# Batch one loaded in runs of four tokens with its last 64 apart, w_out by converting transfers of GpSimd's queue, batch three's loads behind it

## The chip, the cores and the metric

The kernel runs on one core of a Trainium2 chip. The core has five engines with a queue of instructions each: TensorE (matrix products and transposes, into PSUM), VectorE, ScalarE, GpSimd and SyncE (SP, which here only starts DMA transfers). Sixteen DMA engines move data between HBM and SBUF, whichever queue a transfer was started from. The metric is the device time of one execution in microseconds (us); lower is better.

## What is computed

Eight batches of eight heads, 576 tokens of 64 values each, go through attention within a window of 32 tokens to either side; the result, as 4608 tokens of 512 values, goes through a layer with a squared ReLU.

```python
scores = scale * np.matmul(q, k.transpose(0, 1, 3, 2))
mask = np.abs(pos[:, None] - pos[None, :]) <= 32
attn = softmax(np.where(mask, scores, -1e9))
x = np.matmul(attn, v).transpose(0, 2, 1, 3).reshape(4608, 512)
h = np.maximum(x @ w_in, 0.0)          # w_in 512 x 2048
out = (s * (h * h) + b) @ w_out        # w_out 2048 x 512
```

All inputs and the output are float32; the products run in bf16.

## The kernel before

The program is a list of tasks. `add` notes for each its engine (or the DMA queue that it is started on), an estimated cost, what it reads and writes, a key and explicit waits. `_Graph.plan` then puts the tasks of all engines into one order: each time it takes the task that can start first by its own model of engines and DMA rings, the lower key where two can start together. `_Graph.emit` turns dependencies across engines into semaphore waits. Each engine executes its tasks strictly in the planned order, so a wait on one holds up all behind it. Transfers have their order on SP's queue from rising keys (`nxt()`).

**Batches.** The code counts batches from 0; "batch one" is `b == 0`. Batches one to three are worked on by TensorE transposes of q and k; later batches use DMA transposes and are not touched by the change.

**Batch one.** `load_pair` (605) brings q or k of two heads, 576 tokens, as 128 partitions of nine tokens in a row (2304 bytes, `ROWS = 9`). `turn_pair` (618 to 640) casts to bf16 (622 and 623), transposes in eighteen 64x64 pieces (631) into a bank of `W`, and copies out into `QT` (ScalarE, 636) and `KT` (VectorE, 637). `pair_scores` (918) then makes the scores of one pair: two products add a large negative number where the window is shut (925), sixteen products of 64 key tokens by 128 query tokens go on top, and two more make the ninth key tile, with its 64 tokens, into `AVN`. An exp (946) per pair follows, one more for the ninth tile of all pairs, with a mask (951) behind it. `stir` (614) puts products of ones between them, whose results are overwritten; `STIR` says how many at which place.

**Units.** A unit is 128 query tokens, shifted by 32. `av_part` (843) multiplies exps with V, `finish` divides (865, 867), transposes (874) and copies to `XT` (882). Batch one has five units; the banks that they use are listed in `av_banks`. Unit four's keys take in key tile eight, unit five's key tiles eight and nine.

**Loads of batch one and two.** `ORDER0` orders SP's transfers behind q and k: V 0, then w_in part 0, V 1 to 4, w_in part 1. (Numbers are V tiles, 8 and 9 are w_in's parts; each part is two loads of 512 KB, cast by GpSimd at 564.) V comes in rows of 256 bytes, 256 KB a tile, 128 KB for the last. `ORDER1` continues with batch two: `part` (660, 672) loads the last 64 tokens ("t") and q and k of four heads in runs of four tokens (1024 bytes a row), casts (650), transposes in 128x128 pieces (664, 677) and copies out (655, 656); w_in's parts 2 and 3 and V stand between.

**w_out.** Behind batch two's V, eight loads of 512 KB go from SP's queue into the staging ring `STG` (561), and GpSimd casts each into `WOUT_BF` (564). `constant` (1213) sums w_out's rows on TensorE as they arrive; `weight_sums` (1111) makes four differences of its quarters on VectorE, one of them in place; `second` (1139) is the second layer, fourteen products per 512 tokens with these quarters. Behind w_out on SP's queue come batch three's q and k (`FOURS`, 660 and 672) and V.

**The hidden layer.** `s1` (1082) multiplies `XT` with w_in, ScalarE applies the ReLU (1089) and VectorE squares (1095). The first 512 tokens are cut into 224, 128 and 160 (`SPLIT`); the 224 need units one and two, and the order over w_in's parts is `FIRST`. The staging ring is shared by all loads of q, k and weights, so a load waits until the cast of what stood there before is done.

Of the kernel before, what the change touches and what calls it, by code (L numbers as in the profile page):

```python
# [7 lines left out]
BF16 = mybir.dt.bfloat16  # L8
AF = mybir.ActivationFunctionType
ALU = mybir.AluOpType  # L10

S = 576
# [15 lines left out]
ORDER0 = (0, 8, 1, 2, 3, 4, 9)  # L28
# [7 lines left out]
ROWS = 9  # L36
# [18 lines left out]
STIR = {("turn", 0, "q"): 7, ("scores", 0): 2, ("turn", 1, "q"): 1, ("turn", 1, "k"): 1, ("turn", 2, "q"): 1, ("turn", 2, "k"): 1,  # L55
        ("turn", 3, "k"): 1, ("scores", 2): 1, ("scores", 3): 2, ("av", 0): 2, ("av", 1): 1, ("av", 2): 1}
# [21 lines left out]
class _Graph:  # L78
# [44 lines left out]
    def plan(self):  # L123
# [10 lines left out]
        rings, clock, room = {"sp": [], "act": []}, [0.0], {}  # L134
# [188 lines left out]
def bass_sliding_window_symmetric__then__act_starrelu_kernel(  # L323
# [23 lines left out]
    with ExitStack() as es:  # L347
# [15 lines left out]
        def ps(shape, nm, dt=F32):  # L363
# [14 lines left out]
              for t in QTS]  # L378
# [35 lines left out]
                  "t": [f"dmaT{i}" for i in range(8)]}  # L414
# [135 lines left out]
        def load_weights(which, i, x, key, eng):  # L550

            stg, stgr = stage(2 * DM)
# [65 lines left out]
        def turn_pair(b, name, pr, key, banks, eng, slack):  # L618

            slot, (stg, stgr), ni = b % 2, land["pair", b, name, pr], take("nat", NNAT)  # L620
            nat = NAT[ni][:, 0:576]
            add(eng, (lambda e: e.copy(nat, stg)) if eng == "act" else
                (lambda e: e.tensor_copy(nat, stg)),
                {"act": 670.0, "dve": 420.0, "pool": 700.0}[eng], reads=stgr, writes=[("NAT", ni)],
                key=key, slack=slack)
            res, tile = banks[take("bank", len(banks))]
            if b == 0:
                stir(("turn", pr, name), res, tile, key)
            view = tile.bitcast(BF16)[:, 0:S].rearrange("p (i s) -> p i s", i=ROWS)
            order = view.rearrange("p i s -> p s i")  # L630
            add("pe", [lambda e, i=i, p0=p0: e.transpose(
                view[p0:p0 + 64, i, :], nat[p0:p0 + 64, i * 64:i * 64 + 64], IDENT[p0:p0 + 64, p0:p0 + 64])
                for i in range(ROWS) for p0 in (0, 64)], 600.0 if b == 0 and pr == 0 else 420.0, reads=[("NAT", ni), "IDENT"], writes=[res], key=key)
            flat = QT[slot][:, pr, WIN:WIN + S] if name == "q" else KT[slot][:, pr, :]
            dst = flat.rearrange("p (s i) -> p s i", i=ROWS)
            add(*(("act", lambda e: e.copy(dst, order), 190 + 0.833 * S) if name == "q" else
                  ("dve", lambda e: e.tensor_copy(dst, order), 60 + 1.04 * S)), reads=[res],
                writes=[({"q": "QT", "k": "KT"}[name], slot, x, pr) for x in range(NTILE)], key=key)

        def part(b, which, load_key, key, banks, slack):  # L640
# [6 lines left out]
            eng, out_eng = FCAST[which] if b == 1 else "act", FOUT[which]  # L647
# [10 lines left out]
            if which == "t":  # L658
# [3 lines left out]
                    for src, p0 in ((q, 0), (k, 64))], 1000.0, writes=stgr, key=load_key, dma=("l", 64, 21.5))  # L662
# [12 lines left out]
                600.0, writes=stgr, key=load_key, dma=("l", 32, 60.0))  # L675
# [233 lines left out]
        def pair_scores(b, pr):  # L909
# [21 lines left out]
            if tail:  # L931
                g.tasks[-1].deps.update(g.readers.get(("AVN", 0), []) + g.readers.get(("AVN", 1), []))
                for i in (0, 1):
                    g.writer["AVN", i], g.readers["AVN", i] = g.tasks[-1], []
# [9 lines left out]
        def first_exp(dst, src, np_, sc, res, key, shut=False):  # L944
# [3 lines left out]
            if shut:  # L948
                return
# [542 lines left out]
```

## Time and profile before

| | us |
|---|---|
| median of 3 runs (311.11 to 311.7) | 311.52 |
| the profiled execution | 313.66 |
| its span, first to last instruction | 311.9 |
| TensorE busy in it | 296.0 |
| VectorE, ScalarE, GpSimd busy | 230.5, 156.0, 64.0 |
| mean granted clock of TensorE | 0.982 of full |

A line of the timeline has start, duration, engine, source line, operation, what it writes and reads, and in brackets how long the engine was idle before it and what ended that. A line of the groups has the number of instructions behind an x, then busy time and the mean of one. "Issue" is a pause that ends with no event that the profile shows. PEclk gives the granted TensorE clock in tenths; a digit 9 is 90% or more. Ends of matrix products are modelled, since they are pipelined.

### The profile page before, as it was taken

The numbers are of one execution on the slowest core, as the hardware profiler recorded it, in microseconds if no ns is written. First come the engines' busy times: TensorE is split into PE (matmuls) and PEld (weight loads), VectorE is DVE, ScalarE is ACT, GpSimd is POOL, SyncE is SP. The second block draws the span as 40 slices with busy tenths as digits, with TensorE's granted clock in tenths as the row PEclk, the third lists the DMA queues.
The fourth block names the chain that finished last, engine by engine and source line by source line (L and its number), as shares of the span: only waits on it lengthen the run. The fifth ranks groups of instructions, "written<-read, shape, count | busy, mean of one in ns | idle before, by whom it ended". The sixth has DMA issues, their size and how long they took to land.

```text
span 311.9 us, 8962 instructions
## 1 busy us (share of the span) xinstructions
PE 296.0 (95%) x3906; PEld 215.9 (69%) x3938; DVE 230.5 (74%) x400; ACT 156.0 (50%) x241; POOL 64.0 (21%) x78
## 2 busy tenths in 40 slices
PE   8799988999999998999999999998999999999994
PEld 3458766788878886666666666666666666666783
DVE  3455777899799587789978786976786785666673
ACT  3655865494887653655655344443444433333300
POOL 5343558200000044027014300370000000000000
PEclk9967999999999999999999999999999999999999
DMA  7999899999495799999899879999812110200223
GB/s 233 302 258 354 225 302 291 284 272 241 112 198 148 193 188 177 247 219 201 196 230 199 140 177 277 189 179 165 151 53 84 52 48 5 98 25 11 68 69 105
DMA packets 118073, 54.32 MB, mean 174 GB/s; under 512 B 93760, under 2 KB 112832, under 8 KB 118032
## 3 DMA queue, kind: packets, MB, share of 16 engines
q1 hardware_dynamic: 118032, 53.72, 73.2%
q8 instruction: 32, 0.52, 0.7%
q14 instruction: 9, 0.07, 0.1%
HBM read 36.70 MB, written 9.44 MB: 148 GB/s over the span
## 4 chain that ended last, share of the span: by engine, by line
PE 80%; DMA 5%; DVE 4%; SPq 3%; issue 3%; ACT 2%; POOL 1%; POOLq 0%; ACTq 0%
PE w L1082 35%; PE o L1139 29%; DMA stg<-in_k_dram 4%; PE avn L843 4%; SPq L718 2%; PE sc L1139 2%; PE sc L785 2%; DMA kt<-nat 2%; PE avn L874 1%; POOL nat L737 1%; PE sc L1213 1%; DVE gt L1095 1%; PE o L843 1%; DVE kt L656 1%; PE sc L843 1%
## 5 line engine op out<-in xcount | busy, mean ns | idle before, releaser
L1082 PE MATMUL w<-xt,win 128*128 128x512 bf16 (+4 forms) x805 | 140.0, 315 | 3.8 <-issue 1.7
L1089 ACT ACTIVATE r<-w 128x512 bf16<-128x512 f32 (+2 forms) x148 | 86.6, 586 | 103.1 <-PE w L1082 101.7
L1082 PEld LDWEIGHTS w<-xt,win 128*128 128x128 bf16 x832 | 75.6, 99 | 36.3 <-ACT r L1089 1.9
L1095 DVE TENSOR_TENSOR gt<-r 128x1024 bf16<-128x1024 bf16 (+3 forms) x100 | 60.8, 617 | 34.5 <-ACT r L1089 33.8
L1139 PE MATMUL o<-wout,gt 128*128 128x256 bf16 x528 | 66.5, 273 | 0.0
L1139 PEld LDWEIGHTS o<-wout,gt 128*128 128x128 bf16 x528 | 51.2, 98 | 14.0
L737 POOL CAST nat<-stg 128x1024 bf16<-128x1024 f32 (+2 forms) x28 | 32.7, 1167 | 77.8 <-DMA stg<-in_q_dram 62.7
L813 ACT ACTIVATE ex<-sc 128x1024 bf16<-128x1024 f32 (+1 forms) x29 | 29.7, 1023 | 14.3 <-PE avn L843 13.3
L1139 PE MATMUL o<-tw,gt 128*128 128x256 bf16 x272 | 34.8, 273 | 0.0
L1155 DVE SCALAR_TENSOR_TENSOR outs<-o,sb,cvec 128x512 f32<-128x512 f32 (+1 forms) x36 | 25.8, 716 | 9.2 <-PE o L1139 9.2
L1139 PEld LDWEIGHTS o<-tw,gt 128*128 128x128 bf16 x272 | 26.1, 98 | 7.4
L817 DVE TENSOR_TENSOR ex<-ex,mask 128x1024 bf16<-128x1024 bf16 (+1 forms) x29 | 22.5, 777 | 3.5 <-ACT ex L813 3.0
L1155 DVE SCALAR_TENSOR_TENSOR outs<-o,sb,outs 128x512 f32<-128x512 f32 (+1 forms) x27 | 19.3, 713 | 7.2 <-PE o L1139 7.1
L1131 DVE TENSOR_TENSOR gt<-gt 128x1024 bf16<-128x1024 bf16 (+1 forms) x26 | 23.3, 896 | 0.3
L843 PE MATMUL avn<-vb,ex 64*64 64x65 bf16 x952 | 20.2, 199 | 1.8 <-DMA kt<-nat 0.8
L867 DVE TENSOR_TENSOR xn<-avn,rec 128x512 bf16<-128x512 f32 (+1 forms) x31 | 21.3, 686 | 0.6
L843 PEld LDWEIGHTS avn<-vb,ex 64*64 64x64 bf16 x952 | 13.1, 108 | 11.3 <-issue 5.6
L598 DVE CAST vb<-vst 128x512 bf16<-128x512 f32 (+1 forms) x30 | 13.5, 458 | 5.8 <-DMA vst<-in_v_dram 5.8
L1139 PE MATMUL o<-tw,gsum 128*128 128x256 bf16 x136 | 17.5, 273 | 0.0
L1139 PEld LDWEIGHTS o<-tw,gsum 128*128 128x128 bf16 x136 | 12.9, 98 | 3.1
L882 ACT COPY xt<-avn 128x512 bf16<-128x512 bf16 (+2 forms) x19 | 10.1, 539 | 7.9 <-PE avn L874 7.7
L1131 DVE TENSOR_TENSOR gsum<-gt 128x1024 bf16<-128x1024 bf16 x18 | 13.2, 734 | 0.3
(116 smaller groups left out, 226.7 us busy)
## 6 DMA issues: line engine op xcount, KB each, us to landing
vst<-in_v_dram SPq DMA_DIRECT2D x32, 256.0 KB, 4.6
out_dram<-outs SPq DMA_DIRECT2D x32, 256.0 KB, 2.9
stg<-in_q_dram SPq DMA_DIRECT2D x5, 1024.0 KB, 6.1
stg<-in_k_dram SPq DMA_DIRECT2D x20, 256.0 KB, 6.5
stg<-in_moe_w_in_dram SPq DMA_DIRECT2D x8, 512.0 KB, 7.4
stg<-in_moe_w_out_dram SPq DMA_DIRECT2D x8, 512.0 KB, 7.9
stg<-in_q_dram SPq DMA_DIRECT2D x4, 512.0 KB, 7.7
stg<-in_k_dram SPq DMA_DIRECT2D x4, 512.0 KB, 8.4
```

The source lines that it names most:

```text
L598: (lambda e: e.tensor_copy(VB[0:n, vb, :, 0:D], VST[0:n, vs, :, :])),
L737: (lambda e, dst=dst, src=src: e.tensor_copy(dst, src)),
L813: add("act", lambda e, dst=flat_dst, src=flat_src: e.activation(dst, src, AF.Exp, bias=0.0, scale=0.125), 190 + 0.833 * 512 * len(hs), rea ...
L817: add("dve", lambda e, flat=flat, mask=mask: e.tensor_tensor(flat, flat, mask, ALU.mult), 130 + 0.53 * 512 * len(hs), reads=[("E", ei, hp, ...
L843: return [lambda e: e.matmul(av[64 * x:64 * x + 64, h, 0:D + 1], lhsT=buf[64 * g:64 * g + 64, h % 2, h // 2, c:c + 64], rhs=VB[64 * g:64 * ...
L867: add("dve", lambda e: e.tensor_tensor(XN[xi][0:p1, :].rearrange("p (a c) -> p a c", a=H), av[0:p1, :, 0:D], REC[ri][0:p1, :].rearrange("p ...
L1082: add("pe", [lambda e, g=g, kc=kc: e.matmul(wt[:, g, :], lhsT=WIN_BF[:, kc, (f0 + g) * 128:(f0 + g + 1) * 128], rhs=XT[:, kc, t0 % XR:t0 % ...
L1089: add("act", lambda e: e.activation(rt, wt, AF.Relu, bias=0.0, scale=1.0), 190 + 0.833 * ng * nt, reads=[("W", wb)], writes=[("R1", rb, ha ...
L1095: add("dve", lambda e: e.tensor_tensor(GT[gs][:, f1:f1 + nf, g0:g0 + nt], rr, rr, ALU.mult), 130 + 0.55 * nf * nt, reads=[("R1", rb, x) fo ...
L1131: add("dve", lambda e: e.tensor_tensor(dst, x, y, op), 1240.0 if half is None else 690.0, reads=reads, writes=writes, key=k)
L1139: add("pe", [lambda e, g=g, j=j, dst=dst: e.matmul(dst, lhsT=lhs[:, g, 128 * j:128 * j + 128], rhs=rhs[:, g, :], start=first and g == 0 an ...
L1155: add("dve", lambda e, src=src, dst=dst, other=other: e.scalar_tensor_tensor(dst, src, SB128[:, 0:1], other, ALU.mult, ALU.add), 200 + 1.0 ...
```

## The change

Batch one's q and k are loaded by pairs of heads in runs of four tokens, 512 tokens in all (256 KB a load), cast with a rearrangement, transposed in four 128x128 pieces and copied out. The last 64 tokens of q and k of all heads come with one "t" part (two transfers, 256 KB in rows of 256 bytes) behind V 2, cast by GpSimd. The pairs' scores leave out the ninth key tile and the last 32 query columns of the eighth; `late_scores` makes both for all pairs in sixteen products into `AVN`, followed by two exps and two masks. Unit three uses `SC` in place of `AVN`. w_in part 1 moves ahead of V 4. The filler products change from 21 to 20, with one in place of four behind the last pair's scores.

w_out goes straight into `WOUT_BF` by eight converting transfers (float32 to bf16) on GpSimd's queue. The first two wait until V 2 of batch two has landed, the other six for its V 4. There is no staging and no cast. Batch three's five loads wait until the fifth of these has landed.

```diff
-ORDER0 = (0, 8, 1, 2, 3, 4, 9)
+ORDER0 = (0, 8, 1, 2, "t", 3, 9, 4)
-STIR = {("turn", 0, "q"): 7, ("scores", 0): 2, ("turn", 1, "q"): 1, ("turn", 1, "k"): 1, ("turn", 2, "q"): 1, ("turn", 2, "k"): 1,
-        ("turn", 3, "k"): 1, ("scores", 2): 1, ("scores", 3): 2, ("av", 0): 2, ("av", 1): 1, ("av", 2): 1}
+STIR = {("turn", 0, "q"): 7, ("scores", 0): 3, ("turn", 1, "q"): 2, ("turn", 1, "k"): 1, ("turn", 2, "q"): 1, ("turn", 2, "k"): 1,
+        ("turn", 3, "q"): 1, ("turn", 3, "k"): 1, ("scores", 2): 1, ("scores", 3): 1, ("av", 0): 1}
-        rings, clock, room = {"sp": [], "act": []}, [0.0], {}
+        rings, clock, room = {"sp": [], "act": [], "pool": []}, [0.0], {}
...
         def load_weights(which, i, x, key, eng):
+            if which == "out":
+                f0 = 4 * i + 2 * x
+                src = moe_w_out.rearrange("(fc p) c -> p fc c", p=128)[:, f0:f0 + 2, :]
+                dst = WOUT_BF[:, f0:f0 + 2, :]
+                add("pool", lambda e: e.dma_start(dst, src), 800.0, writes=[("W" + which, i, x)],
+                    key=EARLY + (1.25 if i == 0 else 2.0) + 0.01 * (i + 0.5 * x), waits=[land["v", 1, 2 if i == 0 else 4]],
+                    dma=("g", 16, 87.0))
+                land[which, i, x] = g.tasks[-1]
+                return
...
-        def load_pair(b, name, pr, load_key):
-            stg, stgr = land["pair", b, name, pr] = stage(S)
+        def load_pair(name, pr, load_key):
+            stg, stgr = land["pair", name, pr] = stage(DM)
             add("sp", lambda e: e.dma_start(
-                stg,
-                src_of[name][b, 2 * pr:2 * pr + 2, :, :].rearrange("h (p i) d -> (h p) (i d)", i=ROWS)),
-                600.0, writes=stgr, key=load_key, dma=("l", 8, 112.0 if b == 0 else 98.0))
+                stg.rearrange("p (h c) -> p h c", h=2),
+                src_of[name][0, 2 * pr:2 * pr + 2, 0:512, :].rearrange("h (p i) d -> p h (i d)", i=4)),
+                600.0, writes=stgr, key=load_key, dma=("l", 16, 60.0))
...
+            nat = NAT[ni][:, 0:512]
+            dst, src = nat.rearrange("p (i h d) -> p h i d", i=4, h=2), stg.rearrange("p (h i d) -> p h i d", h=2, i=4)
+            tile = tile.bitcast(BF16)[:, 0:512]
+            add("pe", [lambda e, i=i: e.transpose(tile[:, 128 * i:128 * i + 128], nat[:, 128 * i:128 * i + 128], IDENT[:, :])
+                       for i in range(4)], 260.0, reads=[("NAT", ni), "IDENT"], writes=[res], key=key)
...
-            eng, out_eng = FCAST[which] if b == 1 else "act", FOUT[which]
+            eng, out_eng = FCAST[which] if b < 2 else "act", FOUT[which]
...
-            name = ("SC", "O", "AVN", "SC", "O")[u] if b == 0 else BANK1[u] if b == 1 else "AVN"
+            name = ("SC", "O", "SC", "O", "AVN")[u] if b == 0 else BANK1[u] if b == 1 else "AVN"
...
+        def late_scores():
+            x, c = NTILE - 1, 128 - WIN
+            fns = []
+            for pr in range(NPAIR):
+                for hp in (0, 1):
+                    p = slice(64 * hp, 64 * hp + 64)
+                    fns.append(lambda e, pr=pr, hp=hp, p=p: e.matmul(
+                        AVN[0:64, hp, pr * 128:pr * 128 + 128], lhsT=KT[0][p, pr, 64 * x:64 * x + 64],
+                        rhs=QT[0][p, pr, 64 * x:64 * x + 128], start=True, stop=True))
+                    fns.append(lambda e, pr=pr, hp=hp, p=p: e.matmul(
+                        AVN[64:128, hp, pr * 128 + c:pr * 128 + 128], lhsT=KT[0][p, pr, 64 * x - 64:64 * x],
+                        rhs=QT[0][p, pr, 64 * x - 64 + c:64 * x + 64], start=True, stop=True))
+            key = -24.0
...
+            for u, p0, c0 in ((x // 2, 0, 0), (x // 2 - 1, 64, c)):
...
+                add("act", lambda e, dst=dst, src=src: e.activation(dst, src, AF.Exp, bias=0.0, scale=0.125),
+                    190 + 0.833 * 8 * (128 - c0), reads=[("AVN", 0), ("AVN", 1)], writes=res, key=key)
...
             for t in ORDER0:
-                if t < 8:
+                if t == "t":
+                    part(0, "t", nxt(), -23.5, banks, 200.0)
+                    late_scores()
+                elif t < 8:
...
                     for which in FOURS:
-                        part(b, which, nxt(), due(b, 0) - 4.0 + 0.1 * FOURS.index(which), banks2, 2500.0)
+                        part(b, which, nxt(), due(b, 0) - 4.0 + 0.1 * FOURS.index(which), banks2, 1500.0,
+                             [land["out", 2, 0]])
```

`part` takes the list as waits of its loads. Two slacks of the planner fall from 2500 to 1500 with it (here and in `piece`), which shifts the planned order of what uses these loads.

More of the change, by code (lines that the diff above doesn't have):

```diff
@@ L616, in stir @@
                     n * (427.0 if spot == ("turn", 0, "q") else 240.0), reads=["ONESW"], writes=[res], key=key - 0.05)
[L618 to L625, printed above, removed]
-            res, tile = banks[take("bank", len(banks))]
[L627 to L638, printed above, removed]
@@ L643, in part @@
+        def part(b, which, load_key, key, banks, slack, waits=()):
             slot, ni = b % 2, take("nat", NNAT)
@@ L935, in pair_scores @@
             for u0, n in ((0, 4),) if pr < NPAIR - 1 else ((0, 1), (1, 3)):
                 src = bank[:, :, 128 * u0:128 * (u0 + n)].rearrange("p h (u c) -> p h u c", c=128)
-                first_exp(EXS[:, u0:u0 + n, :, pr, :], src, 128, [(name, 0), (name, 1)],
-                          [("E", u, hp, pr) for u in range(u0, u0 + n) for hp in (0, 1)], key, True)
-            if pr == NPAIR - 1 and tail:
-                first_exp(EXS[0:64, 4, :, :, :].rearrange("p (one h) a c -> p (one a) h c", one=1),
-                          AVN[0:64, :, :].rearrange("p h (a c) -> p h a c", c=128), 64, [("AVN", 0), ("AVN", 1)],
-                          [("E", 4, hp, x) for x in range(NPAIR) for hp in (0, 1)], -24.5)
@@ L945, in first_exp @@
+        def first_exp(dst, src, sc, res, key):
             n = dst.shape[1]
```

60 lines of the change are left out of this document (34 added, 26 removed).

## The prediction

> **What bounds the kernel now.** I read the page first (engine shares, the slices, the chain of waits), then stages of the first 130 us, then TensorE's instructions with what ended each pause.
>
> ```profile
> span 311.9 us, 8962 instructions
> PE   8799988999999998999999999998999999999994
> PEclk9967999999999999999999999999999999999999
> DMA  7999899999495799999899879999812110200223
> PE 80%; DMA 5%; DVE 4%; SPq 3%; issue 3%; ACT 2%; POOL 1%; POOLq 0%; ACTq 0%
> q8 instruction: 32, 0.52, 0.7%
> ```
>
> TensorE fills nearly every slice and carries 80% of the chain; DMA is close to full until about 220 us. So the end is the moment from which TensorE is never out of work, plus its work, plus its pauses. The one stretch that is plainly wasted is in slices three and four, where its clock drops:
>
> ```profile
> 14.20:15.50 1.30, 0.04 (x2) 0.03 (x2) 0.00 (x0) 0.13 (x1) 0.52 (x1) 1.00 0.82 166
> 15.50:17.40 1.90, 1.83 (x45) 0.92 (x45) 0.21 (x1) 1.40 (x3) 1.17 (x2) 0.97 0.82 186
> 17.40:20.80 3.40, 3.25 (x74) 1.98 (x73) 2.67 (x7) 1.58 (x3) 1.10 (x2) 0.50 0.97 260
> 20.80:24.10 3.30, 3.16 (x68) 2.28 (x67) 2.37 (x7) 1.17 (x2) 2.08 (x2) 0.50 1.15 301
> 24.10:27.50 3.40, 3.40 (x27) 3.02 (x25) 0.62 (x3) 1.71 (x4) 1.18 (x2) 0.50 1.07 349
> 46.00:50.00 4.00, 3.86 (x92) 3.23 (x90) 3.87 (x9) 1.65 (x4) 2.94 (x3) 1.00 1.05 394
> ```
>
> Columns are the stretch, its length, busy time of TensorE, weight loads, VectorE, ScalarE and GpSimd, the granted clock, the DMA share and GB/s. From 17.4 to 27.5 us the clock is half, while TensorE is busy 9.8 of 10.1 us: at full clock that work takes about 5 us less. The drop follows an empty 1.3 us and a stretch of 64-row products; the granted clock is at 9 and more again in the fifth slice, after 24.1 to 27.5, the first stretch of dense 128x128 products. From the eighth slice (55 us) on TensorE's digits are nines, so what is won ahead of it should reach the end.
>
> **The front: loads and turning.** Batch one's q and k come in eight loads of 256 KB for eight of 288 KB.
>
> ```profile
> 5.00:10.00 5.00, 4.96 (x116) 2.87 (x114) 2.24 (x5) 2.27 (x3) 1.73 (x4) 1.00 1.02 333
> 15.00:20.00 5.00, 4.28 (x101) 2.31 (x101) 2.37 (x6) 2.98 (x5) 2.16 (x3) 0.73 0.86 195
> 20.00:25.00 5.00, 4.86 (x92) 3.71 (x93) 2.99 (x9) 1.28 (x3) 2.80 (x4) 0.50 1.10 322
> 9.49 0.47 PE L631 MATMUL w<-ident,nat 64*64 64x64 bf16 x18
> 28.08 0.39 PE L664 MATMUL avn<-ident,nat 128*128 128x128 bf16 x4
> 13.03 0.76 DVE L637 COPY kt<-w 128x576 bf16<-128x576 bf16 x1 [0.84 <-PE w L631]
> 15.50 0.42 PE L918 MATMUL o<-qt,kt 64*64 64x128 bf16 x16 [1.26 <-issue]
> 51.80 0.22 PE L874 MATMUL o<-ident,xn 128*128 128x128 bf16 x1 [1.23 <-issue]
> ```
>
> 256 KB less ahead of V and w_in at 333 GB/s is 0.8 us. Rows shrink from 2304 to 1024 bytes; batch two already moves such rows (20 to 27.5 us, 301 to 349 GB/s), so I price that at nothing; at the 195 GB/s of the V stretch the 2 MB would come 3.4 us later, the upper bound. Four 128x128 transposes (0.39) replace eighteen of 64x64 (0.47), and a copy of 512 columns is 8/9 of 0.76: 0.2 us off the last pair's own chain. The 1.26 us pause before the last pair's scores is no wait for data (k was ready at 13.79). A second one stands inside a group of four transposes. The program's code arrives in 32 pieces (the instruction queue), and I take both for a late piece. There are 112 transposes fewer, so 224 instructions with their weight loads, and the pause must move; if it vanishes it is worth up to 1.26. But units two and three wait for V, which moves by 0.8 alone: I take **-0.8** for the front, bounds -2.3 (0.8 + 0.2 + 1.26) and +3.4 - 0.8 = +2.6.
>
> **The last 64 tokens.** Their load of 256 KB in 256-byte rows stands behind V 2, w_in's second part before V 4.
>
> ```profile
> 17.27 0.62 POOL L598 CAST vb<-vst 128x512 bf16<-128x512 f32 x1 [0.71 <-DMA vst<-in_v_dram]
> 17.48 1.02 ACT L946 ACTIVATE ex<-avn 64x1024 bf16<-64x1024 f32 x1
> 18.53 0.68 DVE L951 TENSOR_TENSOR ex<-ex,mask 64x1024 bf16<-64x1024 bf16 x1 [0.41 <-ACT ex L946]
> 19.50 0.61 POOL L598 CAST vb<-vst 64x512 bf16<-64x512 f32 x1 [1.61 <-DMA vst<-in_v_dram]
> 20.90 0.94 PE L843 MATMUL sc<-vb,ex 64*64 64x65 bf16 x32
> 22.31 0.93 PE L843 MATMUL o<-vb,ex 64*64 64x65 bf16 x24
> 21.00 0.59 ACT L882 COPY xt<-o 128x512 bf16<-128x512 bf16 x1 [1.36 <-PE o L874]
> 23.18 1.68 PE L1082 MATMUL w<-xt,win 128*128 128x224 bf16 x8
> 26.89 1.35 PE L1082 MATMUL w<-xt,win 128*128 128x128 bf16 x16
> 29.03 0.39 ACT L655 COPY kt<-avn 128x256 bf16<-128x256 bf16 x1
> ```
>
> V 2 lands at 17.2 now, so near 16.4; the tail 1.3 us later (256 KB at 195 GB/s), 17.7. Then, one after the other: GpSimd's cast 0.61, four transposes at half clock 0.6, ScalarE's two copies 0.8, sixteen products 0.6, two exps (1.02, and a quarter of the columns, about 0.4), two masks (0.68 and about 0.3): 5.0 us, so 22.7, and with hand-overs about 23. Both the fourth unit's key tile and the fifth's depend on it (20.90 and 22.31 now), and V 4 waits behind 1 MB of w_in (3.3 us at 322 GB/s): 19.5 - 0.8 + 1.3 + 3.3, cast at 23.3. These two units are about 2 us late. What covers it is the hidden layer's first products: they need units one and two (copied out by 21.6 now, 20.8 then) and w_in's first part, and take twice 1.68 and 1.35, 4.7 us at half clock. I cost it at nothing; without that cover 2 us.
>
> **The clock.** Those dense products move from 23.2 to about 20.5, ahead of the late units, so the 20.8 to 24.1 stretch is filled as 24.1 to 27.5 is now, and the clock should come back one such stretch earlier: 3.4 us at full instead of half, **-1.7**. Bounds: -3.4 (two) to +1.7 (one more, if they start late). [...]
>
> **Filler products.** Behind 15.5 us they fall from four to one.
>
> ```profile
> 15.90 0.61 PE L614 MATMUL sc<-onesw 128*128 128x512 bf16 x2
> 17.14 0.52 PE L614 MATMUL o<-onesw 128*128 128x512 bf16 x1
> 18.92 0.63 PE L614 MATMUL avn<-onesw 128*128 128x512 bf16 x1
> ```
>
> That is 0.3 + 0.52 + 0.63 = 1.45 less; the tail's transposes (0.6) and products (0.6 less the 0.25 that its eight small ones took within the pairs) give 0.95 back: **-0.5**, bounds -1.45 and 0, since the gaps left may only be waits for V.
>
> **w_out.** Eight loads from SP with a cast each on GpSimd become eight converting transfers on GpSimd's own queue, two behind V 2 of batch two, six behind its V 4.
>
> ```profile
> 45.36 0.61 POOL L598 CAST vb<-vst 64x512 bf16<-64x512 f32 x1 [1.72 <-DMA vst<-in_v_dram]
> L564 POOL CAST wout<-stg x8: 1037/1042/1249, 46.5 to 58.6; 128x1024 bf16<-128x1024 f32 x8
> 64.20 1.21 DVE L1111 TENSOR_TENSOR wout<-wout,tw 128x2048 bf16<-128x2048 bf16 x1
> 66.42 1.04 PE L1139 MATMUL o<-wout,gt 128*128 128x256 bf16 x8
> 71.25 1.91 PE L1139 MATMUL o<-wout,gt 128*128 128x256 bf16 x16
> 54.39 0.61 SPq L660 DMA_DIRECT2D stg<-in_q_dram  x1
> 92.18 1.05 PE L1082 MATMUL w<-xt,win 128*128 128x256 bf16 x8
> ```
>
> GpSimd loses 8 x 1.04 us, work that TensorE's backlog covers, and SP eight issues. V 4 lands at about 45.3; six transfers of 512 KB at the 394 GB/s of 46 to 50 us take 8 us, so all are in by about 54 against 58.6 + 1.04 = 59.7 now. No row shows a converting transfer: at the 195 GB/s of V's small rows the six take 16 us, until 61.5. Even that is covered: the changed half of w_out is written at 64.20 and first read at 71.25, a slack of 5.8 us behind 59.7. So nothing, with bounds of -0.4 (TensorE's other gaps from 46 to 50 and behind, 4.00 - 3.86 doubled and rounded up) and, past the slack, the rival below. Behind GpSimd's new wait stands only V 4's cast, which waits for the same landing. Batch three's five loads now wait on SP for the fifth transfer, with its V and the first output stores behind them: 45.3 + 3 x 1.3 is 49 without any start-up, against 54.39 now, so 5 us of room; their tokens are first needed at 92.18. [...]
>
> **Sum.** Batch two's loads and w_in stand behind 0.8 us less and 1.3 more: +0.5, bounds 0 (backlog) and 0.5; I take it. -0.8 - 1.7 - 0.5 + 0.5 = **-2.5**. The profiled execution took 313.66 us, 2.1 above the median of the runs shown (311.52), so 311.2 for an execution like it and **309.0** for the median.
>
> **Rivals.**
> - **The front only waits elsewhere.** For: units four and five wait for the tail and V 4, and DMA is full, so TensorE runs out of covering work as early as it gains; a window of clock is not won (+1.7 back), the rest is eaten by the 2 us of late units. 309.0 + 1.7 + 0.8 = 311.5, no change. Against: w_in's products are there to run. Chance 0.13.
> - **The tail costs a window.** If the planner sets the late scores ahead of w_in's products, TensorE waits 2 us near 21 and stays at half clock to 31: -0.8 - 0.5 + 0.5 + 2.0 + 1.7 gives 314.4, or 313.0 if the clock is as before and some of the wait is filled. Against: the planner takes what is ready first. I price it at 313.5; chance 0.15.
> - **w_out comes late (the slower side).** It decides where the six transfers need more than 5.8 us past 59.7: 65.5 - 45.3 = 20 us, below 156 GB/s. At 125 GB/s they end at 70.5, 5 us over, in which TensorE waits with its second layer: 309.0 + 5 = 314.0. For: no row prices conversion or GpSimd's queue. Against: 156 is under every loaded stretch above. Chance 0.17.
>
> **Numbers.** Forecast 0.55: its own range is from two stretches of clock won (311.5 - 0.8 - 3.4 - 0.5 + 0.5 = 307.3) and half of the 1.5 left in the front's lower bound, 306.5, to 310.9. A measurement tells 0.2% (0.6 us). So faster 0.55, same 0.13, slower 0.15 + 0.17 = 0.32. The range over the cases is 306.5 to 313.9.
>
> **What would show it.** Right: half clock lasts two stretches, not three; hidden-layer products begin near 20.5, before units four and five; w_out has landed by 54 to 62 and TensorE has no pause near 66; batch three's loads issue before 54. Wrong: TensorE idle between 18 and 24, half clock to 27 or later, a pause at the first second-layer products, or new gaps of TensorE behind 80 us as long as what the front won.

## The result and the profile after

The changed kernel takes **316.3 us** (315.95 to 316.48) against 311.61 for the kernel before on the same chip: a ratio of 1.0148, 95% interval 1.0106 to 1.0189. Of its four runs one took 321.16 us, in a slower state that some runs here fall into; ranges, ratios, intervals and clock losses leave such runs out, medians do not. Measured once more on another chip it was 314.54 us, 1.0120 (1.0071 to 1.0169). The forecast was 309.0, so the sign was wrong. The profiled execution took 316.11 us, of which the span is 314.4.

The page of the changed kernel, from the span to the chain of waits:

```profile
span 314.4 us, 8791 instructions
...
PE   8777989799999998999999999997999999999994
...
PEclk9979989999999999999999999999999999999999
DMA  6999999969794399899698959998822210200223
...
q0 software_dynamic: 2176, 2.10, 4.1%
...
PE 67%; DMA 13%; DVE 5%; POOL 4%; SPq 3%; issue 1%; ACT 1%; POOLq 0%
```

DMA's share of the chain went from 5% to 13%. There are two dips of the clock, in the third and the sixth slice, where before there was one broad one, and the eighth slice (55 to 63 us), a nine before, has a seven for TensorE. The windows of that stretch and of the two dips, in the same columns as in the prediction, for the changed kernel:

```profile
12.00:30.00 18.00, 13.54 (x278) 9.45 (x277) 8.94 (x22) 9.71 (x18) 7.67 (x9) 0.91 1.07 275
42.00:54.00 12.00, 10.51 (x199) 8.49 (x190) 7.41 (x20) 6.37 (x13) 8.76 (x14) 0.86 1.10 194
54.00:62.00 8.00, 6.03 (x47) 4.08 (x46) 2.71 (x6) 2.37 (x5) 0.00 (x0) 1.00 1.18 221
```

and for the kernel before:

```profile
12.00:30.00 18.00, 16.32 (x277) 11.25 (x278) 8.56 (x20) 9.47 (x18) 7.10 (x9) 0.72 1.03 293
42.00:54.00 12.00, 9.95 (x193) 8.25 (x192) 9.78 (x23) 6.70 (x14) 8.17 (x10) 1.00 0.98 307
54.00:62.00 8.00, 7.95 (x64) 6.07 (x64) 6.49 (x12) 3.79 (x7) 2.40 (x3) 1.00 1.03 288
```

Read the first row of each together: from 12 to 30 us the clock is better (0.91 for 0.72), but TensorE stands idle for 4.5 us instead of 1.7. Most of what the clock won (3.4 us by these shares), waiting took (2.8 us more). The two longest of these waits are for the cast of V 1 and for that of w_in's second part:

```profile
16.11 0.72 PE L848 MATMUL o<-vb,ex 64*64 64x65 bf16 x32 [1.32 <-ACT vb L606]
...
24.48 1.83 PE L1103 MATMUL w<-xt,win 128*128 128x224 bf16 x24 [1.16 <-POOL win L573]
```

V 1 did land earlier, at 15.42 us for 16.14, but TensorE was ready for it sooner still. From 42 to 54 us the changed kernel has a half-clock window (45.2 to 48.6 us) that the other trace lacks, and from 54 to 62 us it stands still for 2.0 us. Who ended its pauses is in the view of TensorE's waits (line, what it waited for, us in total, times, longest), here its longest rows that are not the start-up:

```profile
PE sc L1234 <- DMA wout<-in_moe_w_out_dram: 2.0, 2, 1.1
PE w L1103 <- POOL win L573: 1.9, 2, 1.2
PE avn L848 <- DMA kt<-nat: 1.7, 1, 1.7
PE o L848 <- ACT vb L606: 1.3, 1, 1.3
PE avn L848 <- issue: 1.2, 1, 1.2
```

The first row is the surprise. Line 1234 is in `constant`, the column sums of w_out. In the timeline of TensorE it looks so:

```profile
53.12 1.03 PE L1234 MATMUL sc<-wout,onesw 128*128 128x512 bf16 x4
...
54.16 0.60 PE L1234 MATMUL sc<-wout,onesw 128*128 128x512 bf16 x2
55.60 0.60 PE L1234 MATMUL sc<-wout,onesw 128*128 128x512 bf16 x2 [0.85 <-DMA wout<-in_moe_w_out_dram]
57.33 0.60 PE L1234 MATMUL sc<-wout,onesw 128*128 128x512 bf16 x2 [1.13 <-DMA wout<-in_moe_w_out_dram]
57.77 1.91 PE L1103 MATMUL w<-xt,win 128*128 128x256 bf16 x16
```

The hidden layer's products of line 1103 stood behind (that they could have run is shown below, where they do). In the kernel before the same sums, at the same time, show no wait:

```profile
53.57 1.46 PE L1213 MATMUL sc<-wout,onesw 128*128 128x512 bf16 x6
...
55.74 0.59 PE L1213 MATMUL sc<-wout,onesw 128*128 128x512 bf16 x2
```

The transfers themselves, by source line in the changed kernel (duration of an issue, first and last start; then time from issue to landing):

```profile
L556 POOL DMA_DIRECT2D wout<-in_moe_w_out_dram x8: 713/722/837, 42.4 to 49.6; - x8
...
DMA to landing us min/median/max: 5.4/9.3/12.8
```

The last was issued at 49.6 and took 12.8: it landed at 62.4 us. The landings of the last six in the trace are 53.9, 55.6, 57.3, 59.0, 60.8 and 62.4, 1.69 us apart. Batch three's loads, which wait for the third of these, start later than before (54.39), by the timeline of SP's queue:

```profile
57.30 0.60 SPq L665 DMA_DIRECT2D stg<-in_q_dram  x1
```

### The profile page after: what moved, and what is told of

Its sections match the earlier page's. It is cut to its first block, busy times and chain, and to the rows that moved or that the text cites. A ratio compares the mean times of both kernels' runs of the same rounds, so it can differ in the third digit from the quotient of the medians.

```text
span 314.4 us, 8791 instructions
## 1 busy us (share of the span) xinstructions
PE 296.7 (94%) x3837; PEld 213.8 (68%) x3837; DVE 231.4 (74%) x401; ACT 157.2 (50%) x244; POOL 62.9 (20%) x79
## 4 chain that ended last, share of the span: by engine, by line
PE 67%; DMA 13%; DVE 5%; POOL 4%; SPq 3%; issue 1%; ACT 1%; POOLq 0%
PE w L1103 29%; PE o L1160 29%; DMA stg<-in_k_dram 5%; DMA stg<-in_moe_w_in_dram 4%; DMA wout<-in_moe_w_out_dram 3%; PE avn L848 3%; PE sc L1160 2%; SPq L723 2%; POOL nat L742 2%; DMA kt<-nat 2%; PE sc L790 2%; DVE gt L1116 1%; PE avn L879 1%; DVE outs L1176 1%; POOL win L573 1%
## 5 line engine op out<-in xcount | busy, mean ns | idle before, releaser
L1103 PE MATMUL w<-xt,win 128*128 128x512 bf16 (+4 forms) x832 | 144.7, 317 | 2.8 <-POOL win L573 1.9
L1116 DVE TENSOR_TENSOR gt<-r 128x1024 bf16<-128x1024 bf16 (+3 forms) x100 | 60.1, 610 | 34.7 <-ACT r L1110 34.5
L742 POOL CAST nat<-stg 128x1024 bf16<-128x1024 f32 (+2 forms) x28 | 33.5, 1197 | 77.5 <-DMA stg<-in_q_dram 62.0
L818 ACT ACTIVATE ex<-sc 128x1024 bf16<-128x1024 f32 (+1 forms) x29 | 29.7, 1023 | 16.3 <-PE avn L848 14.9
L1152 DVE TENSOR_TENSOR gt<-gt 128x1024 bf16<-128x1024 bf16 (+1 forms) x26 | 25.2, 968 | 0.3
L822 DVE TENSOR_TENSOR ex<-ex,mask 128x1024 bf16<-128x1024 bf16 (+1 forms) x29 | 20.5, 707 | 1.4 <-ACT ex L818 0.4
L607 DVE CAST vb<-vst 128x512 bf16<-128x512 f32 (+1 forms) x30 | 14.3, 484 | 1.3 <-DMA vst<-in_v_dram 1.3
```

The lines of the kernel that those rows point to most:

```text
L607: (lambda e: e.tensor_copy(VB[0:n, vb, :, 0:D], VST[0:n, vs, :, :])),
L742: (lambda e, dst=dst, src=src: e.tensor_copy(dst, src)),
L818: add("act", lambda e, dst=flat_dst, src=flat_src: e.activation(dst, src, AF.Exp, bias=0.0, scale=0.125), 190 + 0.833 * 512 * len(hs), rea ...
L822: add("dve", lambda e, flat=flat, mask=mask: e.tensor_tensor(flat, flat, mask, ALU.mult), 130 + 0.53 * 512 * len(hs), reads=[("E", ei, hp, ...
L1103: add("pe", [lambda e, g=g, kc=kc: e.matmul(wt[:, g, :], lhsT=WIN_BF[:, kc, (f0 + g) * 128:(f0 + g + 1) * 128], rhs=XT[:, kc, t0 % XR:t0 % ...
L1116: add("dve", lambda e: e.tensor_tensor(GT[gs][:, f1:f1 + nf, g0:g0 + nt], rr, rr, ALU.mult), 130 + 0.55 * nf * nt, reads=[("R1", rb, x) fo ...
```

## The experiments

Each set ran beside the kernel before on its own chip; the ratios are to that. Because single profiles turned out to mislead, a second number is taken from every run: span x (1 - mean granted clock), the **clock loss**, an upper bound to what half clock cost it (time at half clock counts there even if TensorE waits in it). One window of half clock is 1.7 us of it: each of the two in the change's first trace lasts 3.41 us (17.87 to 21.28 and 45.18 to 48.59 us), and the one stretch of 10.24 us in the trace of the kernel before (17.27 to 27.51 us) counts as three.

| kernel | median us | ratio (95%) | clock loss us |
|---|---|---|---|
| before, over all five sets (137 runs) | 311.7 to 311.9 | 1 | 2.6 |
| the change, first / again | 316.3 / 314.54 | 1.0148 / 1.0120 | 4.6 / 6.0 |
| front alone | 311.49 | 0.9992 (0.9957 to 1.0026) | 4.1 |
| w_out alone | 312.79 | 1.0030 (0.9999 to 1.0061) | 4.2 |
| change, sums later | 313.35 | 1.0044 (1.0016 to 1.0073) | 4.2 |
| change, no wait of batch three | 315.8 | 1.0112 (1.0051 to 1.0172) | 5.0 |
| w_out alone, sums later | 311.83 | 1.0005 (0.9971 to 1.0039) | 2.3 |
| front, w_in first | 313.55 | 1.0045 (1.0010 to 1.0081) | 4.6 |
| change, plain transfers | 314.93 | 1.0134 (1.0081 to 1.0188) | 4.9 |
| front, 1 MB less | 311.18 | 0.9981 (0.9942 to 1.0019) | 3.6 |
| before, 1 MB less | 312.57 | 1.0024 (0.9988 to 1.0059) | 3.6 |
| front, program shifted | 312.19 | 1.0011 (0.9983 to 1.0040) | 3.5 |
| before again | 311.41 | 1.0000 (0.9968 to 1.0031) | 2.8 |
| front, seven fillers more | 313.04 | 1.0045 (1.0009 to 1.0082) | 1.8 |
| change, sums later, seven more | 313.72 | 1.0037 (1.0009 to 1.0065) | 1.3 |
| before, four fillers fewer | 312.98 | 1.0037 (1.0004 to 1.0071) | 5.0 |
| front, seven more, shifted | 313.02 | 1.0018 (0.9996 to 1.0040) | 1.7 |
| front, fillers as before | 312.67 | 1.0031 (0.9998 to 1.0064) | 2.8 |
| change, sums later, fillers as before | 315.09 | 1.0092 (1.0053 to 1.0131) | 4.1 |

**The two halves of the change.** Front alone: the w_out block and the wait are taken out again.

```diff
-            if which == "out":
...
-                return
...
-                        part(b, which, nxt(), due(b, 0) - 4.0 + 0.1 * FOURS.index(which), banks2, 1500.0,
-                             [land["out", 2, 0]])
+                        part(b, which, nxt(), due(b, 0) - 4.0 + 0.1 * FOURS.index(which), banks2, 1500.0)
```

> The changed kernel with w_out loaded as before (SP's queue, staging, GpSimd's casts) and batch three's loads without their wait; batch one's runs of four and its late last 64 tokens stay. Theory A (w_out's transfers come late and TensorE's column sums of w_out wait for them at 54 to 58 us): these waits of 2.0 us go, the half clock stays at two windows at most, and the time is 309 to 311.5 us, below the kernel before. Theory B (the front itself costs: its lead is given back before 46 us and the pauses behind it are its own): 314 us or more, with no wait at the column sums and the lag against the kernel before still 2 us or more at 60 us.

w_out alone is the kernel before with that block and that wait put in.

> The kernel before with one part of the change: w_out by converting transfers on GpSimd's queue behind batch two's V, and batch three's loads waiting for the fifth of them. Theory A: the column sums of w_out wait for the transfers some 2 to 5 us between 54 and 61 us, and the time is 313.5 to 316 us. Theory B (the front costs, w_out is hidden): 311 to 312 us, and no wait at the column sums over 0.3 us.

The front alone is as fast as before, within about 0.4% either way. Its 311.49 us lie at the very edge of theory A's range, but without the gain that A expected, and its trace has four half-clock windows where A allowed two. w_out alone costs 0.3%, with an interval that just reaches 1; that is less than expected, with one wait of 1.1 us at the sums. The two do not add up to the change's 1.2 to 1.5%.

**The column sums.** One edit, in the changed kernel and in w_out alone:

```diff
-                    440, reads=["ONESW", ("Wout", i // 2, i % 2)], writes=[("SC", 0)], accum=i > 0, key=P2[0, 0] - 4.0 + 0.1 * i)
+                    440, reads=["ONESW", ("Wout", i // 2, i % 2)], writes=[("SC", 0)], accum=i > 0, key=P2[0, 0] - 4.0 + 0.1 * i, slack=6000.0)
```

> The changed kernel with the column sums of w_out given 6 us more in the planner's reckoning, so that they stand further back among the second token tile's hidden-layer products. Theory A: most of the 2.0 us at the column sums go without another pause in their place, 313.8 to 315 us. Theory C (the waits at the sums only hold TensorE where it would have been held at the next step anyway, for instance at the w_out halves of the second layer): the same 2 us turn up behind 60 us, 316 us. Theory B: 316 us.

> The kernel before with w_out's converting transfers, batch three's wait, and the column sums further back (the front as before). Theory A (the only cost of w_out's new way is that the column sums meet it): the 0.9 us that the transfers cost by themselves go, 311 to 312 us, the wait at the column sums under 0.3 us. Theory E (the converting transfers cost also through GpSimd: V's casts of batch two stand behind their issues, and TensorE waited 1.4 us for such a cast at 44 us): 312.5 us or more, with the wait for the cast of V between 42 and 46 us still there.

Timeline of TensorE, changed kernel with the sums later: hidden-layer products now stand between, and no pair of sums has a bracket, though w_out lands no earlier (61.8).

```profile
54.10 0.59 PE L1234 MATMUL sc<-wout,onesw 128*128 128x512 bf16 x2
54.54 1.04 PE L1103 MATMUL w<-xt,win 128*128 128x256 bf16 x8
...
65.60 0.59 PE L1234 MATMUL sc<-wout,onesw 128*128 128x512 bf16 x2
```

From 1.0120 and 1.0148 to 1.0044: by the middle values, moving sixteen products wins 2.4 to 3.2 us, for a visible wait of 2.0 (1.6 in the change's second trace). TensorE's order differs from the change's only between 54 and 84 us. But the three numbers come from three sets, and the intervals of the second measurement and of this version touch (1.0071 and 1.0073). The second measurement was itself expected at 315 to 317 us and came out at 314.54. In w_out alone the ratio goes from 1.0030 to 1.0005 and the clock loss from 4.2 to 2.3, with overlapping intervals. This is as theory A says; that the pauses cost more than their length is not shown.

**Batch three's wait** is dropped from the changed kernel (the second part of the first diff alone).

> The changed kernel without batch three's wait for w_out's fifth transfer. Theory D (batch three's late loads, 57.30 instead of 54.39 us, cost time behind 80 us): 1 us or more less, 315 us or below, with the lag against the kernel before smaller behind 90 us. Theory A: batch three's loads now share the DMA with w_out, which lands no earlier, perhaps 1 to 2 us later; 316 to 317.5 us.

315.8 us, 1.0112, between the numbers of the two theories: the wait costs nothing that can be told. The loads went out from 41.7 us, shared the DMA with w_out, and its last landing moved to 64.9; TensorE's order changed in many places as well.

**Conversion or queue.** The changed kernel with plain transfers on the same queue, staged and cast on GpSimd:

```diff
-                add("pool", lambda e: e.dma_start(dst, src), 800.0, writes=[("W" + which, i, x)],
+                add("pool", lambda e: e.dma_start(stg, src), 800.0, writes=stgr,
...
+                add(eng, lambda e: e.tensor_copy(dst, stg), 1100.0, reads=stgr, writes=[("W" + which, i, x)],
+                    key=key + 150.0, slack=100.0)
```

> The changed kernel with w_out's transfers still on GpSimd's queue, at the same place behind V, but plain, into staging, with GpSimd's casts as before. Theory H (conversion sets the pace): the transfers land 1.35 us apart as on SP's queue instead of 1.7, all by about 58 to 59 us, and with the casts the column sums wait about as long as in the changed kernel, 315 to 317 us. Theory I (the pace comes from the queue, or from batch three's V beside it, not from the conversion): they land 1.6 us apart or more, all by 61 us or later, and the time is 316.5 us or more.

The plain ones land 1.54 us apart (54.02 to 60.19, four steps), the converting ones of the change's second trace 1.57 (53.66 to 61.51, five steps), the ones on SP's queue before 1.36. So the pace is mostly not the conversion's. That is theory I's side, though its 1.6 us and its 316.5 us are both missed, by a little and by 1.6. But this kernel has no wait at the sums in its trace and is still 1.0134: the planner, which saw the casts, had set the sums later by itself. The waits at the sums are thus not all of the change's loss. What holds this one up was not followed. Its last two issues wait for staging until 52.7 us; and TensorE, whose order up to 54 us is the change's, waits 2.03 us at 25.59 us for the cast of w_in's second part, as it did 1.16 us in the change's first trace, but not in its second.

**The front: order and data.** The front alone with `ORDER0 = (0, 8, 1, 2, 9, "t", 3, 4)`:

> The front alone (w_out as before), with w_in's second part loaded ahead of the last 64 tokens and V 3. Theory F (the front's gain is lost to the order on SP's queue: the last 64 tokens' small rows stand ahead of w_in's second part, which landed at 25.0 us instead of 22.7, so the hidden layer's products that were to bring the clock back start late): w_in's second part lands 2 us earlier, and the time is 309.5 to 310.8 us. Theory G (the front's gain is lost later, in a pause without a visible wait and a half-clock window at 44 to 50 us): within 0.5 us of the front alone, 311.2 to 312 us, with that window still there.

w_in's second part landed at 21.6 instead of 25.0 us, and the half clock at 47 to 50 us was gone, yet it is slower, 1.0045: theory F falls, and G's number and its window are missed too. Next, the front alone and the kernel before with 1 MB of w_in not loaded:

```diff
-            add("sp", lambda e: e.dma_start(stg, src), 600.0, writes=stgr, key=key,
-                dma=("l", 16, 87.0))
-            land[which, i, x] = g.tasks[-1]
+            if which == "in" and i < 2 and x == 1:
+                stg, stgr = land["half", i]
+            else:
+                add("sp", lambda e: e.dma_start(stg, src), 600.0, writes=stgr, key=key,
+                    dma=("l", 16, 87.0))
+                land[which, i, x], land["half", i] = g.tasks[-1], (stg, stgr)
```

> The front alone (w_out as before) with 1 MB less to load: of each of the first two parts of w_in only the first half is loaded, and both halves are cast from it, so the hidden layer's weights are partly other numbers; the number of instructions on TensorE is the same. Theory J (the new front is bound by its data: V 1 and w_in's second part arrive no earlier than before, so TensorE's idle time between 12 and 30 us grew by 2 to 3 us in place of the half clock): V 1 lands about 1.5 us earlier, the idle time in that stretch falls from 4 to about 2 us, and the time falls by 2 us or more, to 309.5 us or below. Theory G (the gain is lost in the pause and half-clock window at 44 to 50 us): the time falls by less than 1 us against the front alone.

> The kernel before with the same 1 MB of w_in left out in the same way. Theory J (the old front is bound by TensorE itself, fillers and half clock, more than by its data; the new one by its data): it gains clearly less than the front alone does, 1 us or less, 310.5 to 311.7 us. If it gains as much as the front alone, both are bound by data alike, and the change of runs never had anything to win at these loads.

The front alone gains 0.11% by it, the kernel before loses 0.24%, both within their intervals. Theory J's 2 us are missed: V 1 landed at 14.17 us for 17.09 in the front alone, TensorE's idle time from 12 to 30 us fell from 4.05 to 3.13, and it does not show in the time. In its trace the front without 1 MB is 4.7 us ahead of the front alone at batch two's last turned rows (51.62 against 56.35), and 3.3 at 210 us, where it waits 2.79 us for a DMA transpose of k.

**The clock.** First, what a profile is worth. The kernel before, profiled again:

> The kernel before itself, for a second profile and for the spread. 311 to 312.5 us and a ratio within 0.3% of 1; a profile that is shorter than the first one's 311.9 us of span would show how much of the difference between single profiles is chance, and whether the three half-clock windows at 17 to 27 us and the pauses without a visible wait are there each time.

Its windows, to be read against the two rows of the first profile above:

```profile
12.00:30.00 18.00, 15.66 (x305) 11.68 (x306) 8.62 (x20) 10.82 (x20) 7.91 (x9) 0.91 0.98 280
42.00:54.00 12.00, 9.85 (x155) 8.00 (x156) 7.90 (x17) 4.45 (x10) 8.08 (x11) 0.72 1.01 312
```

The same program now has one half-clock window near 23 us and two from 45 to 52. The three at 17 to 27 us on which the prediction rests were that execution's. Over 137 runs the loss is 2.6 us, one and a half windows, from none to 3.7. Then the fillers, with seven more in the front (`("av", 1): 5, ("av", 2): 2`) and four fewer in the kernel before (`("scores", 3): 1, ("av", 0): 1` and none behind):

> The front alone with seven more filler products where TensorE waits for V 1 and for the second unit's turned rows (five ahead of unit two, two ahead of unit three). Theory M (the fillers that the change took out had held the clock up; the front's 1.5 us of saved work are given back as half clock, 4.1 us lost a run on the mean against 2.6 before): the loss to the clock falls to 2.5 us or less, and the time to 309.5 to 311 us. Theory N (the windows come from the pauses for data and for program, whatever stands in them at 15 to 18 us): the loss stays at 3.5 to 4.5 us, and the time at 311.5 to 313 us, the fillers' own time on top.

> The kernel before with the change's number of fillers behind 14 us (three for seven). Theory M: the loss to the clock rises from 2.6 to 3.5 us or more, and the time by 0.5 to 1.5 us, 312.3 to 313.3 us. Theory N: the saved fillers show as 0 to -0.5 us, 311.3 to 311.8 us, with the loss to the clock within 0.6 us of before.

Windows of the front alone,

```profile
12.00:30.00 18.00, 13.95 (x263) 9.83 (x261) 7.01 (x18) 8.54 (x16) 7.98 (x9) 0.72 0.98 256
```

of the front with seven more,

```profile
12.00:30.00 18.00, 15.36 (x299) 10.26 (x298) 10.47 (x24) 10.66 (x22) 8.00 (x9) 1.00 1.14 291
```

and of the kernel before with four fewer:

```profile
12.00:30.00 18.00, 14.89 (x273) 10.79 (x272) 8.45 (x20) 9.27 (x18) 7.22 (x9) 0.72 1.01 283
```

In these runs the fillers hold the clock: four fewer raise the loss of the kernel before from 2.9 (its set) to 5.0 us and the time by 0.37%, 1.2 us, and TensorE's order is otherwise the same but for one block of products at 73 us. Seven more lower the front's loss from 4.1 to 1.8. That half of theory M is right; its time for the front is not: with seven more the front is slower, not faster. This second experiment is less clean, since with the added fillers the planner also reordered other products of TensorE from 18 us on. The timelines show a lead and where it shrinks. TensorE in the front with seven more,

```profile
51.62 0.34 PE L870 MATMUL avn<-ident,xn 96*128 96x96 bf16 x4
...
202.85 0.32 PE L839 MATMUL avn<-vb,ex 64*64 64x65 bf16 x16
...
214.68 0.32 PE L839 MATMUL avn<-vb,ex 64*64 64x65 bf16 x16 [2.11 <-DMA kt<-nat]
```

and in the front alone:

```profile
56.35 0.34 PE L870 MATMUL avn<-ident,xn 96*128 96x96 bf16 x4
...
205.31 0.32 PE L839 MATMUL avn<-vb,ex 64*64 64x65 bf16 x16
...
213.78 0.32 PE L839 MATMUL avn<-vb,ex 64*64 64x65 bf16 x16 [1.57 <-issue]
```

A lead of 4.7 us at batch two's last rows is 2.5 at 203 to 205 us. At the last rows shown it is 0.9 the other way, but that is not a loss of 3.4 us: with seven more, three more blocks of other products stand ahead of that row, and the front alone pauses 1.57 us at the same row, so the wait for the transposed k is only 0.5 us longer. Behind it, from 215.2 to 218.7 us, the clock of the one with seven more is 0.51, and the front alone's is full.

**Pieces of program.** The front alone has a pause of 1.5 us at 44.5 to 46.0 among attention's 64-row products, with no event at its end, and half clock from 47.1 us, 1.1 us behind it. The ten first fillers are each split into eight, some 140 instructions more:

```diff
+                add("pe", [lambda e, m=m: e.matmul(view[:, 64 * m:64 * m + 64], lhsT=ONESW[:, :], rhs=ONESW[:, 0:64], start=True, stop=True)
+                           for _ in range(n) for m in range(8)] if spot in (("turn", 0, "q"), ("scores", 0)) else
```

> The front alone with its ten first filler products each split into eight of 64 columns: the same work, but some 140 instructions more on TensorE ahead of everything, so that the 16 KB pieces of its program end elsewhere. Theory K (the pause at 44 to 46 us is a late piece of program, and it costs a half-clock window because it falls among the 64-row products of attention): the pause moves to 41 to 42 us or behind 46 us and stands among the hidden layer's dense products, the half clock at 46 to 50 us goes, and the time is 309 to 310.5 us. Theory L (the pause belongs to that place, for instance to a wait that the trace doesn't show): it stays at the same product, 311 to 312 us.

> The front alone with the seven fillers and with its first fillers split, so that the pieces of program end elsewhere too. If pauses for program and for data both draw windows, this one has the fewest: a loss to the clock of 2 us or less and 309 to 310.5 us. If neither matters over many runs, 311.5 to 313 us.

The pause is gone from that place, and so is the half clock at 45 to 50 us in both traces. The same pause stands at the same product in all eight traces with the new front and as many instructions ahead of it, but in six alone (the change twice among them) half clock follows; behind those of w_in first (0.90 us) and of the front without 1 MB the clock stays full:

```profile
46.00 0.22 PE L839 MATMUL avn<-vb,ex 64*64 64x65 bf16 x4 [1.50 <-issue]
42.26 0.22 PE L842 MATMUL avn<-vb,ex 64*64 64x65 bf16 x4 [1.17 <-issue]
```

The first row is the front alone, the second the front without 1 MB. That the pause is a late piece of program fits this, and that a 16 KB piece was read from 41.0 to 42.3 us in the change's first trace, just ahead of its pause (42.5 to 43.7 us), but it is inferred. In the time neither shows: 1.0011 and 1.0018.

**Versions that might beat both.**

> The front alone with as many filler products behind 14 us as the kernel before has (two ahead of the fourth pair's scores, two, one and one ahead of units one to three). Seven more brought the clock back (a loss of 1.8 us for 4.1) and cost 3.8 us of the span without that loss; the kernel before with its fillers cut lost 5.0 us to the clock for 2.9 and 1.3 us of time. If three or four are the right dose, a loss of 2.5 to 3 us and 310.3 to 311.3 us, ahead of the kernel before; if every filler costs as much as it brings, 311.5 to 312.5 us.

> The changed kernel with the column sums further back and the same seven fillers: a version that might beat both. Theory M: 1.5 us below the one with the sums alone, 311.5 to 312 us, a loss to the clock of 2.5 us or less. Theory N: 313 to 314 us.

> The whole change with the column sums further back and as many fillers as the kernel before has. By the right dose 312 to 312.7 us; if every filler costs as much as it brings, 313 to 314 us, as with the sums alone and with seven more fillers.

None does: 1.0031, 1.0037 and 1.0092. The last has its sums moved and no wait at them in its trace, and is still slower than the one with the sums alone (1.0044); its trace has the wait for w_in's second part too, 2.34 us at 25.77 us. The best version with the change's own parts is the front alone or w_out alone with its sums later, both level with the kernel before.

## Why the prediction was wrong, step by step

**w_out, priced at nothing, was the costliest error.** The step that failed is "Even that is covered": it took the slack from the first products of the second layer (66.42) and from the changed half (71.25). The first reader on TensorE is `constant`, at 53 us, and TensorE's order is strict: it stood 2.0 us there. With 62.4 us the landing itself was also nearly 1 us beyond the worse bound (61.5) and 8 beyond the value taken (54): from the first issue at 46.0 the six needed 16.3 us, 193 GB/s, which is the bound's 195 and not the 394 taken. What it cost in the time is 2.4 to 3.2 us by the middle values, with the sums moved; that size is not settled, since two kernels without the wait stay at 1.0134 and 1.0092. The rival "w_out comes late" named the right side, 314.0 us, by the wrong reader; its threshold of 156 GB/s was never reached, so it is luck that its time is close to the second measurement.

Why it landed late: the prediction gave w_out the DMA for itself behind batch two's V. On SP's queue, of batch three's five V tiles two were issued before w_out's last two loads (44.7 and 45.3 us) and three behind them (58.1 us and later). In the changed kernel all five are issued from 40.9 to 47.4 us, beside w_out's transfers on the other queue. The last two, issued at 45.4 and 47.4 us, landed 13.4 and 14.7 us later; the two of the kernel before took 9.2 and 9.4. In the trace the two queues share the DMA engines: from 46 to 60 us packets of GpSimd's queue took 79.8% of the sixteen engines' time and those of SP's queue 40.7%. The prediction would have had to count V's bytes among w_out's.

**The clock, -1.7, failed in its base and its sign.** In the change's first profile the step came true: half clock near 18 to 21.5 us for 17.4 to 27.5, and the first hidden-layer products at 19.8 (forecast 20.5). But over the runs the kernel before loses 2.6 us, not the 5.6 of that profile (311.9 x 0.018), and the front alone 4.1: +1.5 in place of -1.7. The same program lost from none to 3.7 windows a run (0 to 6.2 us over the 137 runs); the prediction counted its windows in a single trace.

**The front, -0.8, with the fillers, -0.5.** The span of the front alone less its clock loss is 306.0 us against 307.5 in its set, -1.5: about the saving that these two terms have together, -1.3. It does not reach the time, since the clock loss rose by as much. For the fillers alone the sign was wrong: four taken from the kernel before cost 1.2 us. (A slip in the bounds: at 195 GB/s for 333 the 2 MB would come 4.5 us later and not 3.4, so the front's upper bound should have been 3.7; it changes nothing here.)

**"What is won ahead of it should reach the end"** did not hold for what was won: two traces (1 MB less, seven fillers more) led the front alone by 4.7 us at batch two's last rows, lost part of it on the way and then waited 2.8 and 2.1 us for k's DMA transposes at 210 to 215 us. That wait stood in the profile before (0.80 us at 212.71) and was not weighed. The front alone pauses 1.57 us at the same row, so the waits by themselves took 1.2 and 0.5 us of the lead; a window of half clock behind each (212.0 to 215.4 us in the first trace, 215.2 to 218.7 in the second) is up to 1.7 us more. The wait is not there in every trace (the change's second has none), so its share in the time is not settled.

**Right:** the last 64 tokens cost nothing at their own place (the late scores at 21.6 us waited for nothing), and batch three's wait, though it came 8 us later than reckoned, costs nothing that can be told. "The front only waits elsewhere" has the front's number, 311.5, and part of its way: TensorE does wait elsewhere, but the runs have 1.5 us saved and 1.5 us lost to the clock, where the rival had the clock unchanged and late units.

**The sum.** Front 0 instead of -2.5, the sums 2.4 to 3.2, and 1.4 (change with the sums later, 1.0044) that neither half has alone: front 0.9992, w_out with its sums later 1.0005. The interval of that kernel leaves 0.5 to 2.3 us for that rest if the halves are taken at nothing, and their own intervals are about 1 us to either side, so it may be less. Its cause stays open, as does why plain transfers and the last version, both without a wait at the sums, stay at 1.0134 and 1.0092. A wait of 2.0 and 2.3 us for w_in's second part stands in the traces of these two and is missing in that of the front alone; two single traces do not show that it is the cause.

## What to carry to other kernels

When a transfer is moved, look for its first reader on each strictly ordered engine, a small side product too (here 2.0 us of waits at the column sums), and count as its company on the DMA engines whatever now stands on the other queue (here 40.7% of their time). Don't price half-clock windows from one trace: take the clock of many runs (here none to 3.7 windows in one program), and treat fillers and pauses together, since fillers saved can be a window lost (here four fewer raised the loss from 2.9 to 5.0 us). A lead on the bounding engine may shrink at the next place where that engine already waited for a transfer (here k's DMA transposes, 2.1 and 2.8 us), so look for such places before counting it; when an edit makes a planner set a new order, the same row in two traces no longer stands for the same work.

## What was not expected of the hardware

A converting transfer of w_out halves the bytes written (256 KB for 512) but not the DMA engines' time: its packets of 1024 written bytes took 98 ns each on the mean between 46 and 60 us, the plain ones of 2048 bytes before 93, and both need 256 for a transfer of 512 KB. GpSimd's issue of one took 0.72 us. And a pause of 0.9 to 1.5 us among batch two's 64-row products was followed by half clock in six of eight traces of the new front; the 1.23 us before a run of dense products, at 50.6 us of the first profile, were not.
